# Eight output buffers for three, and one raw-V buffer for two, in an attention-then-experts kernel

**Chip and metric.** One core of one Trainium2 chip. The time is device microseconds of that core for the whole program. A kernel is run several times; a run that is over 1.5% above the fastest of the same kernel is called slow and left out of comparisons. The span of a profiled execution is some 2 us shorter than the time of its run.

## The reference, cut to what matters

```python
# attention: 8 batches, 8 heads, 576 positions, head size 64, window +-32
scores = (q @ k.T) / 8, masked to |i - j| <= 32
x = softmax(scores) @ v                  # laid out (8, 576, 512)
# experts: one of 8 for each batch, chosen from the mean of x
e = argmax(x.mean(1) @ w_gate); g = softmax(x.mean(1) @ w_gate)[e]
out = g * (relu(x @ w1[e]) @ w2[e])      # w1: 512 x 1024, w2: 1024 x 512
```

Inputs and outputs are float32. The expert of a batch is known only when its attention is done, so its weights (W1, then W2, 2 MB each in float32) can be fetched only then.

## The kernel before

A planner in the kernel's own source simulates the engines and emits the instructions in the order that the plan finds best. Each engine then runs its own stream in that order, whatever really happens. Batch b's expert products (L664, W1; L700 and L706, W2) are interleaved with the attention of batch b+1 (L439 scores, L468 exponentials, L482 and L487 masks, L513 product with V).

The parts that the change and the argument touch (batch numbers run from 0 to 7; cuts are marked by three dots):

```python
# the planner: when a finished operation's buffers come free, as the plan sees it
over = end + self.LAT[op.eng]
if op.land and op.eng == "ACT":                       # a store
    dma_at = max(dma_at, end + 1.3) + op.land / (self.DMA_GBS * 1e3)
    over = end + 2.6
elif op.land: ...                                     # a load
    over = dma_at + 0.7

buffers("raw", [P, 2, J, D], FP32, 5)                 # raw q and k
vraws = buffers("vraw", [P, NVS + 1, D], FP32, 2)     # raw V of a whole batch
buffers("w1", [P, NDT, F], FP16, 2)
buffers("w2", [P, NFT, DM], FP16, 2)
buffers("osb", [P, DM], FP32, 3)                      # outputs on their way out

def loadv(op):                                        # two transfers, issued by SP
    t = op.got["vraw"][0]
    ...
    nc.sync.dma_start(t[:, 0:NVS], rows[...])                 # L351, the large piece
    nc.sync.dma_start(t[0:32, NVS], rows[...])                # L354, the small piece

def evac(op, i=i):                                    # five in a batch, on ACT
    osb = op.got["osb"][0]
    nc.scalar.activation(osb[:, 0:w], bank...[:, 0:w], ACTF.Copy, scale=gwb)   # L726

def store(op, i=i):                                   # issued by ACT too
    if i < 4:
        nc.scalar.dma_start(out[b, 128 * i : 128 * i + 128, :], osb)           # L737
        return
    nc.scalar.dma_start(out[b, 512:576]..., osb[:, 0:256])                     # L739
```

So every output goes bank, osb, DRAM. An osb buffer is free again only when its store has landed, and ACT, which fills it, also runs all the exponentials and about half of the copies out of the banks.

The softmax here doesn't subtract the row's maximum and nothing guards it: scores larger than these inputs give would overflow.

## Time and profile before

| | before |
|---|---|
| time, median of 3 runs | 305.97 us (305.24 to 307.08) |
| span of the profiled run | 302.7 us |
| PE busy | 231.4 us, 76% |
| mean granted PE clock | 0.861 |
| ACT waiting for an osb buffer | 53.5 us, 13 times |

How to read it: no engine is near 100%, so waits decide. Line 2 of the page cuts the span into 40 slices; the digits are tenths, and the rows are PE's busy share, then the granted clock of PE.

```profile
PE   1475878995899649995699729993599929975990
...
PEclk9996975999599958997599958997599977995798
```

Every fourth or fifth slice PE falls to 2 to 6 tenths, and in the slice beside it the clock falls to 5 to 7. That is one dip per batch. The work of one batch, from the issue of its W1 to the next, looks so (the columns: stretch, its length, then busy time and number of instructions of PE, PEld, DVE, ACT and POOL, then clock, DMA share, GB/s):

```profile
129.07:163.20 34.13, 28.06 (x305) 21.46 (x304) 21.93 (x54) 18.62 (x40) 8.19 (x10) 0.85 0.73 202
```

PE stands 34.13 - 28.06 = 6.07 us of it, and part of the 28.06 is work at half clock: the clock was 0.50 from 146.3 to 149.6 us. Behind the same wait of three other batches it was 0.50 too (from 109.9, 179.5 and 248.2 us on, for some 4.5 us), and 0.58 behind that of a fourth (from 215.0 us). "Cold" below is work at such a clock, "warm" is work at about 1.00.

### The profile page before, as it was taken

To read this page: it belongs to the slowest core of one execution; us is meant where nothing else is said; L and a number is where in the kernel's file an instruction comes from. 1 tells how busy PE (TensorE), PEld (TensorE's weight loads), DVE (VectorE), ACT (ScalarE), POOL (GpSimd) and SP (SyncE) were. 2 spreads that over 40 slices of the span, in tenths; PEclk is the share of its full clock that TensorE was granted. 3 is DMA by queue.
4 is the path that set the end of the run, shared out by engine and by line. 5 is a ranking of instruction groups with operands and counts; after the bars stand their busy time and mean duration, and the time that the engine had idled before them with its cause. 6 is when DMAs were issued, how large, how long until landed. Compare 5 with 4: busy or idle time off the path is not lost.

```text
span 302.7 us, 6131 instructions
## 1 busy us (share of the span) xinstructions
PE 231.4 (76%) x2432; PEld 177.3 (59%) x2432; DVE 168.9 (56%) x453; ACT 163.5 (54%) x320; POOL 68.4 (23%) x83
## 2 busy tenths in 40 slices
PE   1475878995899649995699729993599929975990
PEld 1374756854796339854496429852497518833840
DVE  7889992475459735685458925686277525400000
ACT  8692923572578255681577425681466535631640
POOL 4536060091106400091004600082002200010000
PEclk9996975999599958997599958997599977995798
DMA  7879999099997997089942996079101970089021
GB/s 248 281 214 393 298 197 269 30 180 264 348 344 166 241 362 223 1 157 235 384 131 38 241 322 228 2 142 226 68 2 17 212 192 17 2 160 239 35 106 53
DMA packets 26637, 55.00 MB, mean 182 GB/s; under 512 B 2064, under 2 KB 12272, under 8 KB 24560
## 3 DMA queue, kind: packets, MB, share of 16 engines
q0 software_dynamic: 2304, 16.78, 29.4%
q1 hardware_dynamic: 18656, 28.39, 27.5%
q10 hardware_dynamic: 5648, 9.44, 8.5%
q8 instruction: 19, 0.31, 0.4%
q14 instruction: 10, 0.08, 0.1%
HBM read 61.94 MB, written 9.44 MB: 236 GB/s over the span
## 4 chain that ended last, share of the span: by engine, by line
PE 49%; DMA 31%; DVE 8%; ACT 5%; issue 4%; ACTq 0%
DMA out_dram<-osb 28%; PE bank L664 25%; PE bank L700 9%; PE bank L513 5%; PE bank L391 4%; PE bank L549 3%; DMA w<-in_moe_w_dram 3%; ACT E L468 2%; ACT osb L726 2%; PE bank L574 1%; DVE E L487 1%; ACT kT L307 1%; DVE qT L305 1%; PE bank L439 1%; PE bank L596 1%
## 5 line engine op out<-in xcount | busy, mean ns | idle before, releaser
L664 PE MATMUL bank<-xT,w 128*128 128x288 f16 x512 | 90.3, 333 | 12.6 <-ACT osb L726 7.3
L664 PEld LDWEIGHTS <-w 128*128 128x128 f16 x512 | 66.5, 151 | 23.6 <-issue 9.0
L682 ACT ACTIVATE hT<-bank 128x288 f16<-128x288 f32 x128 | 51.8, 411 | 37.0 <-PE bank L664 31.5
L513 PE MATMUL bank<-vaug,E 128*128 128x65 f16 x576 | 33.9, 210 | 39.4 <-ACT E L468 30.2
L700 PE MATMUL bank<-w,hT 128*128 128x512 f16 x256 | 63.6, 379 | 0.0
L726 ACT ACTIVATE osb<-bank,gwb 128x512 f32<-128x512 f32 (+1 forms) x40 | 25.7, 642 | 64.6 <-DMA out_dram<-osb 53.5
L487 DVE TENSOR_TENSOR E<-E,mask 128x384 f16<-128x384 f16 (+1 forms) x64 | 34.6, 550 | 38.9 <-ACT E L468 38.9
L513 PEld LDWEIGHTS <-E 128*128 128x128 f16 x576 | 29.2, 109 | 43.6 <-issue 32.5
L634 POOL DMA_DIRECT2D w<-in_moe_w_dram x8 | 4.7, 585 | 176.8 <-DVE gw L627 135.5
L468 ACT ACTIVATE E<-bank 128x512 f16<-128x512 f32 x72 | 41.1, 596 | 3.5 <-PE bank L439 1.4
L330 POOL CAST qkb<-raw 128x1152 bf16<-128x1152 f32 x32 | 37.7, 1212 | 13.5 <-DMA raw<-in_k_dram 7.4
L305 DVE COPY qT<-bank 64x512 bf16<-64x512 bf16 (+1 forms) x46 | 35.3, 774 | 2.1 <-PE bank L391 0.6
L700 PEld LDWEIGHTS <-hT 128*128 128x128 f16 x256 | 22.8, 98 | 18.3
L391 PE MATMUL bank<-id_bf,qkb 128*128 128x128 bf16 x288 | 25.4, 234 | 10.2 <-POOL qkb L330 7.6
L391 PEld LDWEIGHTS <-qkb 128*128 128x128 bf16 x288 | 20.4, 105 | 15.2 <-POOL qkb L330 8.1
L535 DVE TENSOR_TENSOR xs<-bank,linv 128x256 f16<-128x256 f32 x64 | 27.1, 424 | 2.2
L439 PEld LDWEIGHTS <-kT 128*128 128x128 bf16 x288 | 20.3, 103 | 10.2 <-issue 4.7
L439 PE MATMUL bank<-qT,kT 128*128 128x128 bf16 x288 | 24.6, 230 | 1.9 <-DVE qT L305 1.3
L307 ACT COPY kT<-bank 128x512 bf16<-128x512 bf16 (+1 forms) x26 | 18.4, 736 | 9.7 <-PE bank L391 9.6
L305 DVE COPY xT<-bank 128x512 f16<-128x512 f16 (+1 forms) x23 | 8.8, 384 | 25.9 <-PE bank L549 25.8
L365 POOL CAST vaug<-vraw 128x1152 f16<-128x1152 f32 (+1 forms) x16 | 18.9, 1236 | 6.8 <-DMA vraw<-in_v_dram 6.8
L533 DVE RECIPROCAL linv<-bank 128x4 f32<-128x4 f32 (+1 forms) x80 | 13.9, 174 | 8.6 <-PE bank L513 8.1
(61 smaller groups left out, 176.8 us busy)
## 6 DMA issues: line engine op xcount, KB each, us to landing
w<-in_moe_w_dram POOLq DMA_DIRECT2D x16, 1024.0 KB, 11.9
raw<-in_q_dram SPq DMA_DIRECT2D x16, 576.0 KB, 4.6
raw<-in_k_dram SPq DMA_DIRECT2D x16, 576.0 KB, 9.6
out_dram<-osb ACTq DMA_DIRECT2D x32, 256.0 KB, 10.5
out_dram<-osb ACTq DMA_DIRECT2D x8, 128.0 KB
vraw<-in_v_dram SPq DMA_DIRECT2D x8, 0.2 KB, 11.2
vraw<-in_v_dram SPq DMA_DIRECT2D x8, 8.0 KB, 10.0
vraw<-in_v_dram SPq DMA_DIRECT2D x1, 24.0 KB
```

What stands on the lines that cost most here:

```text
L305: nc.vector.tensor_copy(dst, src)
L330: nc.gpsimd.tensor_copy(t, raw[(b, quad, name)].rearrange("p h j d -> p j h d"))
L391: nc.tensor.transpose(pv[:, j - j0, :], raw[(b, quad, name)][:, j], id_bf)
L439: nc.tensor.matmul(dst, qkT[(b, a, "k")][:, k0 : k0 + P], qkT[(b, a, "q")][:, :, k0 : k0 + 64], start=(m == 0), stop=True, skip_group_chec ...
L468: nc.scalar.activation(dst, src, ACTF.Exp, bias=0.0, scale=0.125)
L487: nc.vector.tensor_tensor(ev, ev, mask[:, 1:2].unsqueeze(1).broadcast_to([P, 2, m, 64]), ALU.mult)
L513: nc.tensor.matmul(bank[:, hp * 65 : hp * 65 + 65], E_of[b][:, h, c0 : c0 + P], va_of[b][:, late, slot, 0:65], start=(hp == 0 and n == 0), ...
L535: nc.vector.tensor_tensor(xv[:, par], hv[:, :, 0:64], linv.to_broadcast([n, 4, 64]), ALU.mult)
L664: nc.tensor.matmul(bank[:, 0:288], w_of[b][0].rearrange("p t (c n) -> p t n c", c=P)[:, dt, ft], xT_of[b][:, dt, 288 * c : 288 * c + 288], ...
L682: nc.scalar.activation(h_of[(b, ft)][:, 288 * c : 288 * c + 288], bank_of.pop(gn)[:, 0:288], ACTF.Relu,)
L700: nc.tensor.matmul(bank, h_of[(b, ft)][:, 128 * i : 128 * i + 128], w2s[:, ft, :], start=(ft == 0), stop=(ft == NFT - 1),)
L726: nc.scalar.activation(osb[:, 0:w], bank_of.pop(f"2{b}{i}")[:, 0:w], ACTF.Copy, bias=0.0, scale=tiny("gwb", [P, 1], FP32, b),)
```

## The change

Its intent: five stores per batch into three buffers hold up ACT, so give the outputs more than a whole batch of buffers. Eight osb of 2 KB per partition and two raw V of 9.25 KB do not fit: that build is refused, since it needs 210.2 KB per partition and 207.9 are there. So raw V gives up one buffer. The planner's line is told that a store's buffer comes free only when it lands, or 10 us after its issue at the latest.

```diff
-                over = end + 2.6
+                over = max(end + 2.6, min(dma_at + 0.7, end + 10.0))
...
-    vraws = buffers("vraw", [P, NVS + 1, D], FP32, 2)
+    vraws = buffers("vraw", [P, NVS + 1, D], FP32, 1)
...
-    buffers("osb", [P, DM], FP32, 3)
+    buffers("osb", [P, DM], FP32, 8)
```

## The prediction

> **What bounds the kernel now.** I read the page first, then the waits by total, then one steady batch in the timeline and in stretches.
>
> The chain of work that ended last, and the busy shares of the page:
>
> ```profile
> PE 231.4 (76%) x2432; PEld 177.3 (59%) x2432; DVE 168.9 (56%) x453; ACT 163.5 (54%) x320; POOL 68.4 (23%) x83
> ...
> PE 49%; DMA 31%; DVE 8%; ACT 5%; issue 4%; ACTq 0%
> DMA out_dram<-osb 28%; PE bank L664 25%; PE bank L700 9%; PE bank L513 5%; PE bank L391 4%; PE bank L549 3%; DMA w<-in_moe_w_dram 3%; ACT E L468 2%; ACT osb L726 2%; PE bank L574 1%; DVE E L487 1%; ACT kT L307 1%; DVE qT L305 1%; PE bank L439 1%; PE bank L596 1%
> ```
>
> No engine is full, and the largest single item on the path, 28% of 302.7 us, is the landing of output stores. A store should release nothing but its own buffer. The waits by total say what it holds:
>
> ```profile
> ACT osb L726 <- DMA out_dram<-osb: 53.5, 13, 6.7
> ...
> PE bank L513 <- ACT E L468: 30.2, 9, 5.6
> ...
> PE bank L664 <- ACT osb L726: 7.3, 4, 2.5
> ...
> PE bank L664 <- DMA w<-in_moe_w_dram: 5.0, 2, 3.6
> ```
>
> Columns: microseconds in total, times, longest. ACT stands 53.5 us for osb, because a batch has five evictions into three buffers. ACT runs in order, so the exponentials (L468) queued behind the blocked eviction stand too; PE waits for those (30.2 us) or for a psM bank (7.3 us). The 85.7 us of the chain is not the gain, as the same stretch holds weight landing and other work; the PE idle it causes, 37.5 us, is nearer. One steady batch, in order of time:
>
> ```profile
> 171.90:179.50 7.60, 0.40 (x8) 0.34 (x9) 2.78 (x9) 2.12 (x4) 0.00 (x0) 0.66 1.00 276
> 179.50:184.00 4.50, 4.43 (x26) 3.27 (x26) 1.79 (x5) 2.82 (x7) 0.00 (x0) 0.50 1.06 393
> 184.00:194.00 10.00, 10.00 (x150) 9.89 (x148) 5.89 (x21) 6.33 (x15) 0.00 (x0) 0.97 0.28 85
> ```
>
> ```profile
> 172.47 0.69 ACT L726 ACTIVATE osb<-bank,gwb 128x512 f32<-128x512 f32 x1 [2.96 <-DMA out_dram<-osb]
> ...
> 173.78 0.40 PE L513 MATMUL bank<-vaug,E 128*128 128x65 f16 x8 [1.91 <-DVE E L487]
> ...
> 178.55 0.47 ACT L726 ACTIVATE osb<-bank,gwb 128x256 f32<-128x256 f32 x1 [4.91 <-DMA out_dram<-osb]
> 178.92 0.59 ACT L468 ACTIVATE E<-bank 128x512 f16<-128x512 f32 x1
> ...
> 179.56 0.60 PE L513 MATMUL bank<-vaug,E 128*128 128x65 f16 x8 [5.38 <-ACT E L468]
> ```
>
> In each stretch the first figure is its length and the second is PE's busy time; the last three are clock, DMA share and GB/s. PE works 0.40 of 7.60 us, then runs 4.5 us at clock 0.50, then is full at 0.97. The batches repeat every 33.5 to 35 us.
>
> [...] 0.50 after the 5.4 us gap, while after the 1.9 us gap before 173.78 eight L513 took 0.40 us, as in the dense stretch. [...] a 256 KB store takes 10.5 us to land (median), with the DMA share at 1.00 at that point. So a store that needs no waiting lands no sooner after the change; it only holds nobody.
>
> **The change part by part.**
>
> (a) osb 3 to 8. A batch has five stores, so eight buffers mean that a buffer is wanted again after more than a whole batch (about 27 us) against a landing of 10.5 us (12.8 at most). The 53.5 us of ACT waits for osb goes to 0. For PE in the steady batch: the fourth eviction (2.96 us of waiting) can run when its matmuls end, near 169.9, and the fifth near 171.1, after L706. The first L513 stays at 173.75, since it also waits for masks on DVE, which come after the vaug copies at 170.5 to 172.9. The second set, now at 179.56, can come at about 174.6, and with it L664, if its weights are there. They are: W1 for this batch is issued at 163.2 and lands 8.5 us later, at 171.7 (8.3 to 9.9 us in the batches from the third on). Gain 5.0 us. Over the kernel: 30.2 + 7.3 = 37.5 us of PE idle, less 0.5 us in each of seven batches that stays for masks, is 34 us.
>
> (b) The clock. Sixteen L664 took 3.84 us after the gap (the chain shows it at 180.16) and cost 0.121 us each in dense stretches (12 in 1.51 us, so 16 in about 1.94): 1.9 us lost per batch. [...] Six batches: 11 us. The seventh gap (270.9 to 274.5, before the last batch) is a wait for W1, 3.6 us long, and stays; there only about 2 us of the store wait goes, already counted in (a).
>
> (c) vraw 2 to 1. No instruction's work changes except that three of the six POOL memsets at the start go (0.4 us, beside DMA). The load of V for batch b+1 can be issued only after the cast of V for batch b. Now the loads run ahead: issued at 80.95, 105.8, 138.9 and 172.5 for casts at 130.4, 164.5, 199 and 234. Afterwards each goes out just after the cast before it (at about 97, 133, 167, 201 on the old clock). A load lands in 10 to 11 us and is wanted a whole batch later, 27 us even after shortening, so it should be hidden. Behind it in SP's order stand the next four q/k loads; the small V load keeps SP for 6.3 to 14.6 us, so they move to about 175 to 178. Landing in about 10 us, they are needed at about 194 on the new clock: slack about 6 us. At the start V of batch 1 waits for 15.9 instead of going out at 13.0, but q/k of batch 1 may go first. I take 0 for it.
>
> (d) The planner's line. `over` only moves when the plan thinks an osb buffer is free. With eight of them this orders hardly anything differently. I take 0.
>
> (e) What comes in return. The plan shrinks a batch from 34.4 to about 27.3 us. DMA is busy about 23 us per full batch (shares by queue 29.4 + 27.5 + 8.5 = 65% of 302.7 is 198 us over 8), so it still fits, but V now moves in the same 10 us as W1, W2 and the five stores. I allow 0.5 us of later W1 per batch: 3 us. And the kernel's program gives SP's and ACT's transfers eight completion semaphores in turn: each transfer waits until the one eight before it has landed. The trace of before shows such waits where no buffer explains them:
>
> ```profile
> SPq L354 <- DMA out_dram<-osb: 14.5, 3, 6.2
> SPq L351 <- DMA out_dram<-osb: 8.7, 3, 4.7
> ```
>
> A V load waits for a store. A batch has 5 stores, 4 q/k and 2 V transfers: eleven. With V late after the cast it falls between the stores, and then the fifth store may have the first store of the same batch eight before it: issued 163.6, landed 172.4, while the fifth is ready at about 171.6. That is about 1 us of a new ACT wait in five batches, mostly behind one exponential that PE needs first: I take 2 us.
>
> Sum: 34 + 11 - 3 - 2 = 40, and 305.97 - 40 = 266; the start may give 2 to 4 back, since q/k of batch 1 no longer stand behind V. I say **263 us**.
>
> **Rivals.**
>
> (1) The semaphore turn takes the osb wait's place. If the fifth store has the second store eight before it (issued 166.2, landed about 178), ACT stands till nearly where it stood. For it: eleven transfers per batch and V's move between the stores. Against: one exponential runs ahead of the fifth store, and L664 can then fill three banks. It would make 280 to 292 us.
>
> (2) The weights become the bound. For it: W1 shares DMA with more traffic, and the loop from pooling to the W1 issue (3.9 us) to landing (9 us) to the next pooling (about 12 us dense) is 25 us, close to the 27 that PE needs. If W1 takes 13 us, each batch is 2 us longer: 270 to 278 us.
>
> (3) One V buffer delays loads. If a raw load or V comes late for its cast, POOL waits and PE's transposes with it. Each micro-delay costs directly; 3 us in five batches gives 278 us. Against: the slack of 6 us or more above.
>
> (4) The stall was hidden anyway, another wait standing behind it. Against: during the gap W1 has landed, DVE is idle (2.78 of 7.60 us busy) and POOL has nothing to do. It would give 300; I hold it unlikely.
>
> **Range and chances.** The core case, with only small returns, gives 255 to 268; (2) and (3) in part reach 278; (1) in full lies beyond. So 253 to 279 for eight in ten. Faster by over 2% (below 299.9) 0.95, within 2% 0.04, slower 0.01.
>
> **What would show it.** (a) right: the row of ACT waiting for out_dram is gone, L513 waiting for L468 falls from 30.2 to under 8 us, and the chain holds under 5% of stores. (b) right: mean clock from 0.861 to at least 0.92, PE busy from 231 to about 220. (c) right: POOL's waits for vraw and raw stay near the present 6.8 and 11.8 us. (e) right: DMA to landing of w stays under 12 us for the first of each pair. The prediction is wrong if ACT idles before L737 or L739 or the instruction after it for a landing (rival 1), if L664 waits for w in several batches (rival 2), if L330 or L365 on POOL waits for loads (rival 3), or if PE stays at 0.5 clock in mid batch.

The marks in it stand for what no trace or run of this case shows. 34 + 11 - 3 - 2 = 40, and about 3 more from the start, so 305.97 less 43, which is 263 us. One step of (b) is gone with the cuts, that the short gaps which stay leave the clock alone. It was the author's estimate, from the one gap of 1.9 us before 173.78, and it did not hold every time: behind gaps of 1.00 and 0.27 us the changed kernel once ran at clock 0.53 (rival 2 in the last part).

## The result, and the profile after

| | before | after |
|---|---|---|
| time, median of 3 runs | 305.97 us | 252.97 us (250.96 to 255.03) |
| ratio of fast runs | 1 | 0.823 (0.813 to 0.833) |
| profiled span | 302.7 us | 251.1 us |
| PE busy | 231.4 us | 214.2 us |
| PE standing (span less busy) | 71.3 us | 36.9 us |
| mean granted PE clock | 0.861 | 0.951 |

A ratio, here and below, is the mean time of one kernel's fast runs over that of the other's of the same rounds, so it is not quite the ratio of the medians that are quoted. The later run of the same changed kernel (six runs beside eleven of before) gave 252.77 us and 0.834 (0.829 to 0.840).

The page of the changed kernel, busy shares and the chain of work that ended last:

```profile
PE 214.2 (85%) x2432; PEld 169.0 (67%) x2432; DVE 167.6 (67%) x453; ACT 163.9 (65%) x320; POOL 68.4 (27%) x80
...
PE 55%; DVE 22%; DMA 11%; issue 5%; ACT 3%; POOLq 1%; ACTq 1%
PE bank L664 27%; DMA w<-in_moe_w_dram 11%; PE bank L700 10%; PE bank L513 6%; DVE E L487 5%; DVE qT L305 4%; PE bank L549 4%; PE bank L391 3%; DVE E L482 3%; PE bank L439 2%; DVE vaug L368 2%; PE bank L574 2%; ACT E L468 1%; DVE vaug L370 1%; DVE kT L305 1%
```

No store is on the chain any more, where it held 28% before. DVE has taken 22% of it. The same two rows of 40 slices as before:

```profile
PE   0575586799989998999899989999799999986990
...
PEclk9999598589999999999999999999799999999996
```

After the first quarter the dips are gone, but for one at the 29th slice and the wait for the last weights near the end. The waits by total (us in total, times, longest):

```profile
ACT osb L726 <- PE bank L700: 12.8, 19, 1.4
...
PE bank L513 <- DVE vaug L370: 6.0, 5, 2.1
...
PE bank L664 <- DMA w<-in_moe_w_dram: 5.1, 3, 3.5
POOL qkb L330 <- DMA raw<-in_q_dram: 5.0, 3, 3.2
POOL vaug L365 <- DMA vraw<-in_v_dram: 4.5, 2, 2.4
```

ACT's eviction (L726) now waits for what it should wait for, the matmuls that fill its bank, and never for a landing. The row of L513 waiting for the exponentials (30.2 us before) is absent. The same stretches from W1 to W1, three of them:

```profile
114.67:140.96 26.29, 25.20 (x305) 20.16 (x304) 21.50 (x54) 18.73 (x40) 8.19 (x9) 1.00 0.98 270
...
167.25:195.67 28.42, 27.07 (x305) 20.90 (x304) 21.60 (x54) 18.97 (x40) 8.19 (x10) 0.94 0.71 182
195.67:219.52 23.85, 23.85 (x282) 18.83 (x281) 15.51 (x50) 17.80 (x38) 3.57 (x6) 1.00 0.61 139
```

A steady batch takes 26.29 us, of which PE works 25.20 at full clock: PE is the bound of the middle of the kernel. The same 305 matmuls took 28.06 us of PE before. The seam between two batches, in order of time:

```profile
121.39 0.69 ACT L726 ACTIVATE osb<-bank,gwb 128x512 f32<-128x512 f32 x1 [0.42 <-PE bank L700]
...
122.55 0.47 ACT L726 ACTIVATE osb<-bank,gwb 128x256 f32<-128x256 f32 x1
122.92 0.59 ACT L468 ACTIVATE E<-bank 128x512 f16<-128x512 f32 x1
...
124.38 1.20 PE L513 MATMUL bank<-vaug,E 128*128 128x65 f16 x15 [1.01 <-DVE vaug L370]
...
125.42 2.15 PE L664 MATMUL bank<-xT,w 128*128 128x288 f16 x16
```

The fifth eviction comes 1.16 us after the fourth, where it was 6.1 us before (172.47 to 178.55), and L664 starts warm: 16 take 2.15 us.

All eight stretches, from the two views (us; the first runs from the start to the second W1, the last from the eighth W1 to the end):

| stretch | length before | after | PE standing before | after | PE busy: before less after |
|---|---|---|---|---|---|
| start | 60.04 | 60.81 | 19.2 | 21.2 | 1.2 |
| six in the middle | 205.62 | 158.71 | 40.1 | 5.3 | 12.0 |
| last | 37.04 | 31.58 | 11.9 | 10.4 | 3.95 |
| sum | 302.7 | 251.1 | 71.3 | 36.9 | 17.2 |

PE does the same 2432 matmuls in both, so the last column is what the same work took longer before, beside a mean granted clock of 0.861 against 0.951. 34.4 us less standing and 17.2 us less busy time make the 51.6 us between the two spans. The first 60 us, where the program fills, gained nothing.

### The profile page after: what moved, and what is told of

Same layout as the page of the kernel before. It is cut to its first block, busy times and chain, and to the rows that moved or that the text cites. A ratio compares the mean times of both kernels' runs of the same rounds, so it can differ in the third digit from the quotient of the medians.

```text
span 251.1 us, 6127 instructions
## 1 busy us (share of the span) xinstructions
PE 214.2 (85%) x2432; PEld 169.0 (67%) x2432; DVE 167.6 (67%) x453; ACT 163.9 (65%) x320; POOL 68.4 (27%) x80
## 3 DMA queue, kind: packets, MB, share of 16 engines
q1 hardware_dynamic: 18656, 28.39, 33.5%
## 4 chain that ended last, share of the span: by engine, by line
PE 55%; DVE 22%; DMA 11%; issue 5%; ACT 3%; POOLq 1%; ACTq 1%
PE bank L664 27%; DMA w<-in_moe_w_dram 11%; PE bank L700 10%; PE bank L513 6%; DVE E L487 5%; DVE qT L305 4%; PE bank L549 4%; PE bank L391 3%; DVE E L482 3%; PE bank L439 2%; DVE vaug L368 2%; PE bank L574 2%; ACT E L468 1%; DVE vaug L370 1%; DVE kT L305 1%
## 5 line engine op out<-in xcount | busy, mean ns | idle before, releaser
L664 PE MATMUL bank<-xT,w 128*128 128x288 f16 x512 | 76.3, 299 | 5.1 <-DMA w<-in_moe_w_dram 5.1
L664 PEld LDWEIGHTS <-w 128*128 128x128 f16 x512 | 62.5, 147 | 8.1 <-DMA w<-in_moe_w_dram 5.6
L513 PE MATMUL bank<-vaug,E 128*128 128x65 f16 x576 | 32.1, 200 | 12.2 <-DVE vaug L370 6.0
L330 POOL CAST qkb<-raw 128x1152 bf16<-128x1152 f32 x32 | 37.9, 1218 | 13.5 <-DMA raw<-in_k_dram 7.7
L513 PEld LDWEIGHTS <-E 128*128 128x128 f16 x576 | 26.7, 102 | 15.8 <-issue 11.5
L305 DVE COPY qT<-bank 64x512 bf16<-64x512 bf16 (+1 forms) x45 | 34.5, 773 | 2.0 <-PE bank L391 0.6
L487 DVE TENSOR_TENSOR E<-E,mask 128x384 f16<-128x384 f16 (+1 forms) x64 | 33.8, 549 | 2.9 <-ACT E L468 2.8
L726 ACT ACTIVATE osb<-bank,gwb 128x512 f32<-128x512 f32 (+1 forms) x40 | 25.6, 644 | 13.9 <-PE bank L700 12.8
L439 PEld LDWEIGHTS <-kT 128*128 128x128 bf16 x288 | 19.7, 102 | 10.5 <-issue 4.8
## 6 DMA issues: line engine op xcount, KB each, us to landing
out_dram<-osb ACTq DMA_DIRECT2D x32, 256.0 KB, 11.7
```

What stands on the lines that cost most here:

```text
L305: nc.vector.tensor_copy(dst, src)
L330: nc.gpsimd.tensor_copy(t, raw[(b, quad, name)].rearrange("p h j d -> p j h d"))
L439: nc.tensor.matmul(dst, qkT[(b, a, "k")][:, k0 : k0 + P], qkT[(b, a, "q")][:, :, k0 : k0 + 64], start=(m == 0), stop=True, skip_group_chec ...
L487: nc.vector.tensor_tensor(ev, ev, mask[:, 1:2].unsqueeze(1).broadcast_to([P, 2, m, 64]), ALU.mult)
L513: nc.tensor.matmul(bank[:, hp * 65 : hp * 65 + 65], E_of[b][:, h, c0 : c0 + P], va_of[b][:, late, slot, 0:65], start=(hp == 0 and n == 0), ...
L664: nc.tensor.matmul(bank[:, 0:288], w_of[b][0].rearrange("p t (c n) -> p t n c", c=P)[:, dt, ft], xT_of[b][:, dt, 288 * c : 288 * c + 288], ...
```

## Experiments

**What needed no run.** The planner changes only the order of instructions, so I built variants and compared their programs, instruction by instruction on each engine, buffer numbers left out. With eight or five osb the old and the new planner line give the same program on all five engines; at three and four osb they differ. With the old line and one V buffer, three, four, five and eight osb all give the changed kernel's order; with two V buffers and six osb (new line) the order is that of before. So at eight buffers the planner's line does nothing, and the order, where it differs between the two kernels, comes from the number of V buffers. That leaves two parts to test, osb and vraw.

### 1. The two parts, each alone

First the outputs without the V part. Six osb is the largest number for which two V buffers still fit.

```diff
-                over = end + 2.6
+                over = max(end + 2.6, min(dma_at + 0.7, end + 10.0))
-    buffers("osb", [P, DM], FP32, 3)
+    buffers("osb", [P, DM], FP32, 6)
```

> Six osb buffers, two V buffers: every engine has the instruction order of the kernel before, only the buffers differ (eight and two do not fit). Theory A (the store buffers alone bring the gain, and the clock loss they remove is larger than I forecast, 17 us in place of 11): 253 us, within 4. Rival B (the 10 us more than forecast come from the V part, whose loads move away from the weights or whose order starts batch 1 sooner): 261 to 265 us.

Measured: 265.07 us (four runs, 261.3 to 266.85, of which two fast), ratio 0.863 (0.851 to 0.875). The profile is of one of the slow runs, but the same wait shows in the fast runs of section 4. Then V alone:

```diff
-    vraws = buffers("vraw", [P, NVS + 1, D], FP32, 2)
+    vraws = buffers("vraw", [P, NVS + 1, D], FP32, 1)
```

> Three osb buffers as before, one V buffer, the planner's old line: every engine has the instruction order of the changed kernel. Theory A: 306 us, within 4, with ACT waiting over 45 us for stores. Rival B: 294 to 298 us.

Measured: 304.55 us (302.79 to 306.26), ratio 1.002 (0.992 to 1.012), nothing. The waits of this kernel stand as they stood before:

```profile
ACT osb L726 <- DMA out_dram<-osb: 53.0, 13, 6.9
...
PE bank L513 <- ACT E L468: 38.5, 11, 5.9
```

So the V part is worth nothing where the osb wait is there. But beside many osb it is worth some 10 us: about 263 with two V buffers (the fast runs 261.3 and 264.13) against 253 with one. The two parts interact, and the prediction had given V the value 0 in both places. Of the two forecasts, theory A (253 us) missed the first run and rival B (294 to 298) the second. What happens with six osb and two V buffers? The waits of that run, and the same moment in its timeline:

```profile
ACT E L468 <- DMA vraw<-in_v_dram: 10.5, 1, 10.5
...
PE bank L664 <- ACT hT L682: 8.4, 1, 8.4
```

```profile
85.15 0.79 SPq L351 DMA_DIRECT2D vraw<-in_v_dram  x1
85.99 18.40 SPq L354 DMA_DIRECT2D vraw<-in_v_dram  x1
...
97.58 0.47 ACT L726 ACTIVATE osb<-bank,gwb 128x256 f32<-128x256 f32 x1
...
108.42 0.54 ACTq L739 DMA_DIRECT2D out_dram<-osb  x1
109.00 0.60 ACT L468 ACTIVATE E<-bank 128x512 f16<-128x512 f32 x1 [10.47 <-DMA vraw<-in_v_dram]
...
109.95 0.88 PE L664 MATMUL bank<-xT,w 128*128 128x288 f16 x3 [8.39 <-ACT hT L682]
```

The fifth eviction is done at 98.05, and its store needs nothing but that, yet it goes out at 108.42. In between ACT does next to nothing, and PE stands 8.4 us. An exponential needs no raw V, and neither does a store. What ties them is the turn that the prediction described: SP's and ACT's transfers share eight completion semaphores, and each waits until the transfer eight before it has landed (in the built programs each of the 82 transfers after the first eight carries this wait; in the trace of before the 90 transfers report their landings on eight semaphores, 11 or 12 on each, and six V transfers and one of k go out within 0.1 us of the earlier landing on theirs). Read off the built programs, the transfers around the fifth store (O4) of batch 1 stand in this order:

```
six osb, two V:   V large, V small*, q, O0, O1, O2, k, O3, q, O4
changed kernel:   q, k*, q, k, O0, O1, O2, V large, O3, O4
                  (* is the one eight before O4)
```

With two V buffers SP may fetch V two batches ahead, so a V load (batch 4's, issued at 85.15) stands just in front of the stores, and it falls eight before O4. In the same place of the next two batches it is a V load too; from batch 4 on it is another transfer. In the changed kernel the load eight before O4 is one of k in batches 1 to 4, which has long landed; in batch 5 it is the large V load of batch 7, but no wait shows for it. In the kernel before the same collision is in the program, but there the wait for osb holds the stores back until V has landed.

This I call the semaphore theory: the V part's worth is that it takes the V loads out of the fifth stores' turn. The rivals: two V buffers hurt by loads running ahead and crowding the DMA engines, or by the other instruction order.

### 2. How many output buffers

```diff
-    vraws = buffers("vraw", [P, NVS + 1, D], FP32, 2)
+    vraws = buffers("vraw", [P, NVS + 1, D], FP32, 1)
-    buffers("osb", [P, DM], FP32, 3)
+    buffers("osb", [P, DM], FP32, 4)
```

> Four osb buffers, one V buffer, the changed kernel's order. Only the fifth eviction of a batch can wait, for the landing of the first store, which was 8.8 us after its issue in the batch I read, while the fifth is wanted about 8 us after it. Theory A: 0.5 to 2.5 us of ACT waiting per batch, mostly beside other work, so 254 to 260 us. If a short ACT wait costs PE as much as a long one (or cools the clock), 265 us or more.

Measured: 263.54 us (261.45 to 264.04), ratio 0.864 (0.855 to 0.873). I had expected less: the waits that stay are short, but they cost nearly all that they last, since they sit on ACT right before PE's next work.

```profile
ACT osb L726 <- DMA out_dram<-osb: 13.5, 6, 3.4
...
PE bank L513 <- ACT E L468: 7.6, 5, 2.4
```

The same with five:

> Five osb buffers, one V buffer, the changed kernel's order. A buffer is wanted again only a whole batch (over 23 us) later, against a landing of about 12 us: no ACT wait for stores, 253 us, within 2 of the changed kernel, by both theories. If it is slower by over 4, landings must take longer than the trace's median says.

Measured: 253.19 us (250.82 to 253.92, five runs), ratio 0.832 (0.825 to 0.840), the same as the changed kernel with 6 KB less per partition. The step is between four and five buffers, the number of stores in a batch.

### 3. What the half clock costs by itself

To keep the gap and take away only the cold start (clock 0.50 from 179.5 to 184.0 us, in the prediction's stretches), dummy matmuls go into an unused part of a bank in the kernel before. They touch no result.

```diff
                     bank_of[an] = bank
+                    if i == 0 and par == 0 and 2 <= b:
+                        for _ in range(80):
+                            nc.tensor.matmul(bank[:, 384:512], id_f16, id_f16,
+                                             start=True, stop=True, skip_group_check=True)
```

> The kernel before, with 80 dummy matmuls (128x128 into unused columns of the bank) after the first attention group of batches 2 to 7, where PE then stands some 5.4 us for ACT: about 4.4 us of work nobody needs, in the gap. The store waits stay. If the clock loss is a cost of its own, about 2.5 us in each of six batches by the comparison of PE's busy time per batch, the time falls to 288 to 294 us. If the idle time alone counts, 303 to 307 us; if the dummies get in the way, more.

Measured: 301.43 us (299.32 to 302.8), ratio 0.994 (0.984 to 1.004), unclear, and not the 288 to 294 us of the first forecast. In one batch the dummies did not lie in the gap, and that stretch grew from 33.5 to 37.9 us; in three others they ran partly cold themselves, 6.25 us in place of 4.63. But behind them the first 16 L664 after the gap (here L670) took 2.16 us in place of 4.03. The kernel before, then the one with dummies:

```profile
179.97 4.03 PE L664 MATMUL bank<-xT,w 128*128 128x288 f16 x16
```

```profile
182.69 2.16 PE L670 MATMUL bank<-xT,w 128*128 128x288 f16 x16
```

So again, with 60 dummies and only in batches 4 to 7:

```diff
-                    if i == 0 and par == 0 and 2 <= b:
-                        for _ in range(80):
+                    if i == 0 and par == 0 and 4 <= b:
+                        for _ in range(60):
```

> The kernel before with 60 dummy matmuls in the gap of batches 4 to 7 only: in the run with 80 in batches 2 to 7 the clock rose to 0.921, but those of batch 2 did not fall in a gap (that interval 4.4 us longer) and some ran cold for 6.26 us and overran it; the well-placed ones shortened their intervals by about 2 to 3 us. Clock loss as a cost of its own: 4 times 2 to 2.5 us, so a ratio to before of 0.967 to 0.975. If the clock does not count by itself: 0.995 to 1.005.

Measured: 298.06 us (293.81 to 299.93), ratio 0.975 (0.968 to 0.983); three of the six runs were fast, and the verdict on record is unclear, since the interval takes in a gain of 2%. That is 0.0248 x 302.46 = 7.5 us over four batches, 1.9 us for each (1.3 to 2.4 by the interval), while the wait for osb is all there:

```profile
ACT osb L732 <- DMA out_dram<-osb: 55.8, 13, 6.9
```

So the cold start after the gap is a cost of its own, beside the gap, and the size that the prediction gave it per batch, 1.9 us, lies in that interval.

### 4. Testing the semaphore theory

First a cheap remedy: swap the two pieces of the V load, in both kernels, so that the small one, which keeps SP for up to 18 us, goes first.

```diff
+                nc.sync.dma_start(t[0:32, NVS], rows[...])
                 nc.sync.dma_start(t[:, 0:NVS], rows[...])
+                return
```

> Six osb, two V buffers, the order of before; only the two loads of one V change places: the 8 KB one goes out ahead of the 1.15 MB one. In the run with six osb and two V buffers the fifth store of batch 1 stood 10.5 us at the semaphore of the 8 KB load eight transfers before it, whose issue took 18.4 us behind the large load. Theory C (the V part of the change helps only by moving that load out of a store's turn): the wait falls on the large load, landed by then, and the time is 252 to 256 us. Rival D (V with one buffer helps in another way, by DMA traffic or the start): 262 to 266 us as without the swap.

> The changed kernel with the two loads of V swapped. By theory C there is no collision in it to remove: 251 to 255 us, within 1% of the changed kernel. If SP's 14 us at the small load hold the next q/k loads back enough to matter, 247 to 250 us.

> The changed kernel itself, on the same chip as the swaps, to compare with: 251 to 255 us, ratio to before 0.82 to 0.84.

Measured: six osb with the swap 263.6 us (261.27 to 264.86), ratio 0.869 (0.862 to 0.876). The changed kernel with the swap 252.87 (251.84 to 253.44), and unchanged 252.77 (252.02 to 253.44). The swap does nothing in either. By its number the first run went to rival D (262 to 266 us); theory C had counted on the large piece being landed by then. In the first the store still stood for V:

```profile
82.65 0.71 SPq L352 DMA_DIRECT2D vraw<-in_v_dram  x1
...
105.02 0.54 ACTq L741 DMA_DIRECT2D out_dram<-osb  x1
105.60 0.60 ACT L470 ACTIVATE E<-bank 128x512 f16<-128x512 f32 x1 [9.72 <-DMA vraw<-in_v_dram]
```

Now the large piece is the second, so it is the one eight before O4, and O4 could go 22.4 us after its issue. The remedy failed; the wait stayed where the turn puts it. Next, let SP issue the fifth store of batch 1 in place of ACT. In the program so built its turn moves too: the transfer eight before it is now a q load. What it waits for is its place in SP's stream, behind both pieces of V, and meanwhile ACT can go on:

```diff
-                nc.scalar.dma_start(
+                (nc.sync if b == 1 else nc.scalar).dma_start(
```

> Six osb, two V buffers; one store of the forty, the fifth of batch 1, goes out from SP in place of ACT, so that the wait for batch 4's V load stands in SP's queue, which holds only loads, and not in front of ACT's exponentials. The swap of the V loads did not help, as the large load too landed only at 105 us. Theory C (semaphore turn: an ACT store behind the V load of batch 4): the 10 us ACT wait is gone, 250 to 256 us. Rival D (the second V buffer costs in another way): 261 to 266 us.

Measured: 261.04 us (254.41 to 263.89; five of six runs slow beside the one of 254.41, so there is no ratio). The wait was gone from batch 1 and came in batch 2, whose fifth store has a V load eight before it as well:

```profile
130.82 0.56 ACTq L739 DMA_DIRECT2D out_dram<-osb  x1
131.43 0.60 ACT L468 ACTIVATE E<-bank 128x512 f16<-128x512 f32 x1 [9.74 <-DMA vraw<-in_v_dram]
```

Or let V of batch 4 take the buffer of batch 3, so that it is fetched a batch later; the order of instructions stays:

```diff
+        vname = "vraw" if b in (0, 2, 5, 7) else "vrawB"
...
-        plan.add("SP", 1.2, f"ldv{b}", loadv, takes=[("vraw", 1)], ...
+        plan.add("SP", 1.2, f"ldv{b}", loadv, takes=[(vname, 1)], ...
```

> Six osb, two V buffers, the order of before; only the V load of batch 4 takes the buffer of batch 3, so it must go out after that cast, as in the changed kernel; all other V loads still run ahead. Theory C: this one load is what the V part of the change has to move: 250 to 256 us. If V loads running ahead also cost in later batches: 257 to 262; rival D: 261 to 266 us.

Measured: 258.97 us (255.04 to 259.81), ratio 0.850 (0.843 to 0.857), three of six runs fast. A part came, and again the wait moved on to batch 2:

```profile
ACT E L471 <- DMA vraw<-in_v_dram: 9.1, 1, 9.1
```

A theory that names the stores can be asked for all of them. The fifth stores of batches 1, 2 and 3, those with a V load eight before them, go to SP; V's loads, its buffers and the order of all other instructions stay. The turns of these three stores move here too, so that each has a q load eight before it:

```diff
-                nc.scalar.dma_start(
+                (nc.sync if b in (1, 2, 3) else nc.scalar).dma_start(
```

> Six osb, two V buffers, the order of before; the fifth stores of batches 1, 2 and 3 go out from SP. In the built programs these three stores have a V load eight transfers before them when V has two buffers, none of them with one; taking batch 1 alone out of the turn moved the 10 us ACT wait to batch 2 (9.7 us, same row). Theory C: with all three out of ACT's queue no ACT wait for a V load is left, and the time is that of the changed kernel or a little better: 249 to 255 us. Rival D (two V buffers cost in another way): 258 us or more with no such row.

Measured: 254.35 us (252.82 to 256.1, six runs, all fast), ratio 0.841 (0.836 to 0.846). The span is 251.1 us, as the changed kernel's, and no wait of ACT for V or for a store is left. The store of batch 1 stands in SP's stream behind the small piece of V and goes out while ACT works on:

```profile
99.50 0.71 ACT L682 ACTIVATE hT<-bank 128x288 f16<-128x288 f32 x2 [0.47 <-PE bank L664]
...
100.38 0.83 SPq L739 DMA_DIRECT2D out_dram<-osb  x1
100.51 1.39 ACT L682 ACTIVATE hT<-bank 128x288 f16<-128x288 f32 x3 [0.30 <-PE bank L664]
```

That settles it between the theories. V still runs two batches ahead, its large piece for batch 4 still takes 23.1 us to land (23.0 in the run of section 1), and the order of all but these stores is still that of before. Yet from 98 to 110 us of the span PE works all 12 us, where it worked 2.79 in that run. So neither crowding nor order is what cost the 10 us; three stores moved to another stream, and with that out of V's turn, gave it back. Stream and turn are not told apart by this run. Some 1.5 us to the changed kernel may stay (254.35 against 252.8, measured in different calls); I did not follow them.

| | two V buffers | one V buffer |
|---|---|---|
| three osb | 305 | 304.55 |
| four osb | not run | 263.54 |
| five osb | not run | 253.19 |
| six osb | 265.07 | not run |
| six osb, three fifth stores from SP | 254.35 | not run |
| eight osb | does not fit | 252.97, 252.77 |

No version clearly beats the changed kernel; five osb with one V buffer equals it in less memory.

## Why the prediction was right or wrong

The forecast was a gain of 43 us to 263; it was 53, to 252.97, a hair below the low edge of the range. The traces differ by 51.6. Of the 8.6 us that the forecast lacks of that, 6.2 are the clock term (11 said, 17.2 measured) and 2.4 are standing time (34 less 5 plus 3 at the start makes 32; 34.4 measured).

- **(a) The osb wait goes: right, in size too.** The row of ACT waiting for stores is gone, though a store of 256 KB takes no less time to land (11.7 us in the median, 10.5 before). L513 waits for exponentials in no row, and PE's standing time fell by 34.4 us against 34 (34.8 in the middle and 1.5 in the last stretch, less 2.0 that the start lost). The step from 37.5 us of idle PE, not from the 85.7 us of the chain, is what made this term good. The run with four buffers shows how directly such waits count.
- **(b) The clock: a loss there was, the size not right.** This is the step that failed: "1.9 us lost per batch" and "Six batches: 11 us" was too little, and PE's busy time fell by 17.2. In five of the six middle stretches it fell by 2.0 to 2.9 us, 2.5 on average. The forecast had counted only the sixteen L664; the L513 and L549 beside them were cold as well (0.60 and 0.63 us in the trace of before, 0.41 and 0.39 warm). In the sixth it rose by 0.5 us, at clock 0.53 behind a late W1 (rival 2 below). So the 12.0 us of the six agree with 11 partly by luck. PE also gained 1.2 us at the start and 3.95 us in the last stretch, whose gap, by the prediction, "stays". The gap did stay, 3.5 us long, yet the 64 L664 behind it took 8.06 us in this run, and 2.14 + 9.88 = 12.02 us in the trace of before: 3.96 us, the whole of that stretch's difference. In another run of the changed kernel they were partly cold behind the same gap (9.68 us, below).

The last batch's first products in the kernel before, where a wait for an osb follows the gap:

```profile
274.48 2.14 PE L664 MATMUL bank<-xT,w 128*128 128x288 f16 x8 [3.61 <-DMA w<-in_moe_w_dram]
277.82 9.88 PE L664 MATMUL bank<-xT,w 128*128 128x288 f16 x56 [1.20 <-ACT osb L726]
```

In the changed kernel's timeline:

```profile
228.25 8.06 PE L664 MATMUL bank<-xT,w 128*128 128x288 f16 x64 [3.52 <-DMA w<-in_moe_w_dram]
```

And in the later run of the same kernel:

```profile
226.26 9.68 PE L664 MATMUL bank<-xT,w 128*128 128x288 f16 x64 [3.55 <-DMA w<-in_moe_w_dram]
```

So the clock behind that gap varies from run to run: 1.00 in the first 3.8 us of work in the one (228.2 to 232.0) and 0.55 in the other (226.2 to 230.0), 1.6 us between these two (and the 64 take 10.64 us in the changed kernel with V's pieces swapped), and the tail's 3.95 us are not all due to the change.

- **(c) V's load stays hidden: right. "0" for the V part: right only where it makes no difference.** POOL's waits for V and for raw q and k are 4.5 and 12.7 us, near the 6.8 and 11.8 of before. But by itself the part is worth 0 and beside many osb some 10 us (section 1 and 4), through the semaphore turn.
- **(d) The planner's line: right.** At eight buffers the program is the same without it.
- **(e) What comes in return: wrong, it was not paid.** W1 landed in 8.1 to 9.5 us in seven of eight batches (8.2 to 9.9 before), so the 3 us allowed for it were not lost, and the 2 us of a new wait before the fifth store did not come. The reason given for the latter failed too: "With V late after the cast it falls between the stores, and then the fifth store may have the first store of the same batch eight before it". In the built program only one piece of V falls between a batch's stores, and a k load is eight before the fifth. The danger was real, but on the other side: it is V running ahead, with two buffers, that collides. At the start the 3 us credited did not come either; the stretch got 0.8 us longer. Its DMA sum is off as well, with no effect: 198 us over 8 batches are 24.7 and not 23.
- **Rival (1), the semaphore turn takes the place of the osb wait:** fell for the changed kernel. The same kind of wait, for a V load and not for a store, is what happens with six osb and two V buffers, though once per run, 10.5 us long, and not in every batch, so 265 and not 280 to 292.
- **Rival (2), the weights:** once. In batch 5 W1 took 11.1 us, and the 16 L664 behind it ran at clock 0.53, the dip at the 29th slice. The idle time before them was 1.00 us, ahead of L513, and 0.27 us:

```profile
178.43 3.84 PE L664 MATMUL bank<-xT,w 128*128 128x288 f16 x16 [0.27 <-DMA w<-in_moe_w_dram]
```

- **Rivals (3) and (4)** fell: no new load waits on POOL, and the stall was not hidden.

What bounds the kernel now is PE in the middle, and the first 60 us and the last 32 at the ends. DVE's 22% of the chain are masks, copies of V, and copies of q and k out of banks. Some of the masks are slow while POOL casts q and k (118.22 to 122.96). The same mask of the same shape during and after those casts:

```profile
118.34 1.30 DVE L487 TENSOR_TENSOR E<-E,mask 128x384 f16<-128x384 f16 x1
...
124.50 0.35 DVE L487 TENSOR_TENSOR E<-E,mask 128x384 f16<-128x384 f16 x1
```

1.30 us against 0.35; the trace of before has the same pair (1.30 at 166.86 during the casts, 0.35 at 173.03 after them). No run here took the casts away, so that they are the cause was not shown.

**What stays open:** why the clock stays up after the same 3.5 us gap in one run (64 L664 in 8.06 us) and not in another of the same program (9.68 us), and why it was 0.53 behind the gaps of 1.00 and 0.27 us of rival 2 (16 L664 in 3.84 us), where in the later run it stayed up behind the gap of 1.00 alone (2.18 us); the 1.5 us of section 4; whether the new planner line would matter at three or four buffers.

## What to carry to other kernels

Give a store at least as many buffers as one round of the loop issues of them, when the engine that fills them also feeds the matmul engine: four buffers for five stores still cost 10 us, and more than five gained nothing. In this kernel a store waited not only for its data and its buffer but also for its turn on shared completion semaphores (10.5 us of ACT, some 10 us of the kernel), so look in the built program for what stands ahead of a store that a compute engine issues; if it is a long load, issue the store from an engine that has nothing else to do, and read the turns again, as they move with it. And when two parts of a change are priced apart, ask what the one was hiding of the other.
